# Attention into two MoE layers on one core: the inverse row sums reach the transposed layout as columns written by GpSimd and whole transpositions, in place of broadcast products

## The chip, the cores and the metric

The kernel runs on one core of one Trainium2 chip. The metric is the device time of one execution in microseconds (us), the median of several runs; lower is better. The names of the engines in the profile are PE (TensorE), DVE (VectorE), ACT (ScalarE), POOL (GpSimd) and SP (SyncE, which only issues transfers here).

## The reference

Three layers follow each other. A thresholded softmax attention over 4 batches, 8 heads, 576 positions and 64 channels feeds a mixture of experts (top 2 of 8), and that feeds a second one (top 1 of 8, with a skip). Only the attention is touched:

```
scores = scale * np.matmul(q, k.transpose(0, 1, 3, 2))
thresh = np.max(scores, axis=-1, keepdims=True) - tau
scores = np.where(scores >= thresh, scores, -1000000000.0)
scores = scores - np.max(scores, axis=-1, keepdims=True)
attn = np.exp(scores)
attn = attn / (np.sum(attn, axis=-1, keepdims=True) + 1e-09)
return np.matmul(attn, v).astype(np.float32)
```

## The kernel before

**Tiling of the attention.** Two heads form a pair, 16 pairs g in all, each with queries in tiles of 128 rows. A unit is one tile of one head, the fifth and last unit-tile holds the last 64 queries of both heads ("mixed"). Chunk c = 0 of a pair has four units, chunk c = 1 has five: nine units a pair, 144 in all. The loop over units is written by hand, as a software pipeline, and every engine executes what it is given in that order.

**One unit.** PE multiplies queries and keys into the score tile `s` (L290, issued two units ahead; three such tiles exist). DVE takes the negated maximum (L298), ACT the exponential (L300), DVE thresholds and sums (L329, tile `P`, or `Pm` for the mixed unit, with the sums at the side). PE transposes the 512 first keys of `P` in four pieces into the one PSUM tile `tp` (L339), which ACT copies to `pt` (L341, for the mixed unit L343). As there is one `tp` tile, the next transpositions wait until that copy is done.

**The end of a chunk.** A chunk of two tiles and two heads has four sums a row, five with the mixed unit. DVE reduces them (L348, `sums1`) and inverts them one unit later (L352, `sums2`). Two units after the chunk's last one, PE does `extra` (L357 to L365): the last 64 keys of both heads stand side by side in columns 512 to 640 of `P`, and are transposed together (L362); the inverse sums have to stand along the columns, so PE multiplies a broadcast inverse sum with the identity (L364, two halves of 64 output rows for each tile). ACT copies both into `rr` (L365). For c = 1 `extra_mixed` (L367 to L375) does the same for the mixed unit, in the `tp` tile, with four products of 64 columns and one ACT copy (L375). Then the products with the values (L386, `av` for four pieces of keys, L389 for the last keys) sum into the PSUM tile `x`, and DVE multiplies by the inverse sums (L396, `norm`).

**What sets the order.** The tables `AV` and `NORM` (L731 to L733) give, for each chunk, the unit and the phase ("mid", "pe", "end") in which the parts of `av` and `norm` are issued. Beside the units, generators are advanced one step at a time: `prep` (POOL multiplies the keys of a later pair by the scale, L273, when their transfer has landed), the router of the first MoE layer (`gate1`), whose results POOL scatters row by row to DRAM (L169, each after a small memset L168), and gathers for the first experts (L177). There are three bursts of such scatters inside the attention: 8, 10 and 8 of them. After the attention come the expert layers (L607, L847), where POOL takes part of the weight splits and the scatters of the output.

Of the kernel before, what the change touches and what calls it, by code (L numbers as in the profile page):

```python
# [8 lines left out]
F32 = mybir.dt.float32  # L9
F32R = mybir.dt.float32r  # L10
I32 = mybir.dt.int32
AF = mybir.ActivationFunctionType
# [5 lines left out]
B, H, S, D = 4, 8, 576, 64  # L18
# [21 lines left out]
def attention_moe_moe(ctx, tc, qT, kT, vm, vr, tau, wgn, noise, w1a, w2a, wsg, w1b, w2b, out):  # L40
    nc = tc.nc
# [11 lines left out]
    ident = const.tile([128, 128], F32, name="ident")  # L53
# [148 lines left out]
    def pool(stack, name, bufs, side="left", **kw):  # L202
        return stack.enter_context(tc.tile_pool(name=name, bufs=bufs, side=side, reuse_waits="tile", **kw))
# [13 lines left out]
    e_p = pool(actx, "e", 3, "right")  # L217
    pt_p = pool(actx, "pt", 2, "right")
    sm_p = pool(actx, "sm", 4, "right")
# [5 lines left out]
    def bank(nm):  # L225
        return banks[0](nm)
# [53 lines left out]
    chunk = {}  # L280
# [31 lines left out]
    def emit_stt(u):  # L312
        g, c, t, hh = UNITS[u]
        s, nm, e, th = st.pop(u)
        if (g, c) not in chunk:
            ch = chunk[g, c] = {}
            ch["pt"] = pt_p.tile([128, 4, 2, 320], F32, name="pt")
            ch["rr"] = pt_p.tile([128, 2, 320], F32, name="rr")
            ch["sums"] = smz[(2 * g + c) % 3]
            ch["P"] = {}  # L320
        ch = chunk[g, c]
        if t < 4:
            if hh == 0:
                ch["P"][t] = e_p.tile([128, 2 * S], F32, name="P", bufs=4)
            o, a = ch["P"][t][:, hh * S:(hh + 1) * S], ch["sums"][:, (t % 2) * 2 + hh, 0:1]
        else:
            ch["P"][t] = e_p.tile([128, S], F32, name="Pm", bufs=1)
            o, a = ch["P"][t], ch["sums"][:, 4, 0:1]
        nc.vector.scalar_tensor_tensor(o.rearrange("p (a b) -> p a b", a=2), s, th, e, op0=OP.is_ge, op1=OP.mult,  # L329
                                       accum_out=a)  # L330

# [16 lines left out]
        nc.vector.tensor_reduce(ch["sm"][:, :4 + c], ch["sums"][:, :4 + c], axis=AX.X, op=OP.add)  # L348

    def sums2(g, c):  # L350
        sm = chunk[g, c]["sm"][:, :4 + c]
        nc.vector.reciprocal(sm, sm)  # L352

    def wide(g, c, k):
        return chunk[g, c]["sm"][:, k:k + 1].to_broadcast([128, 64])

    def extra(g, c):  # L357
        ch = chunk[g, c]
        ps = ps_x.tile([128, 2, 256], F32, name="ex", tag="x")
        for i in range(2):  # L360
            cols = slice(i * 128, (i + 1) * 128)
            nc.tensor.transpose(ps[:, 0, cols], ch["P"][2 * c + i][:, 512:640], ident)  # L362
            for hh in range(2):
                nc.tensor.matmul(ps[hh * 64:(hh + 1) * 64, 1, cols], wide(g, c, 2 * i + hh), ident, start=True, stop=True)  # L364
        nc.scalar.activation(ch["rr"][:, :, 0:256], ps, AF.Copy)  # L365

    def extra_mixed(g):  # L367
        ch = chunk[g, 1]
        rr = ch["rr"]
        ps = bank("em").rearrange("p (k c) -> p k c", k=4)  # L370
        for i, l in enumerate((ch["P"][4][:, 512:S], wide(g, 1, 4))):
            for hh in range(2):
                h = slice(hh * 64, (hh + 1) * 64)
                nc.tensor.matmul(ps[h, i, 0:64], l, ident[:, h], start=True, stop=True)
        nc.scalar.activation(rr[:, :, 256:320], ps[:, 0:2, 0:64], AF.Copy)  # L375

    def av(g, c, kt):
        b, p = PAIRS[g]
# [345 lines left out]
    def early_mm1(k):  # L724
        if k < AHEAD:
            drain(products(e0a, k, ps_s.tile([128, 2, 512], F32, name="s")))
        if 0 < k <= AHEAD:
# [1 line left out]


    AV = (((3, "pe"), (3, "pe"), (4, "pe"), (4, "end"), (5, "pe")),  # L731
          ((3, "pe"), (3, "pe"), (4, "mid"), (4, "pe"), (5, "pe")))
    NORM = ((7, "mid"), (6, "pe"))  # L733
    pq.append(prep(1))
    for u in range(NU):
        g, c, t, hh = UNITS[u]
# [27 lines left out]
        run(u, "pe")  # L764
        run(u, "end")
        emit_stt(u)
        step(pq)
        step(bg)
        if u % 4 == 3:
            step(fq)  # L770
        if (t, hh) == ((1, 1) if c == 0 else (4, 0)):
            k = (g, c)
            sums1(*k)
            at(u + 1, "mid", sums2, *k)
            at(u + 2, "pe", extra, *k)
            if c:
                at(u + 2, "pe", extra_mixed, g)
            for kt, (d, ph) in enumerate(AV[c]):
                at(u + d, ph, av, *k, kt)
            at(u + NORM[c][0], NORM[c][1], norm, *k)  # L780
            if k in GATES:
                at(u + 7, "end", bg.append, gate_and_rows(*GATES[k]))
                if k[0] == 11:
                    at(u + 7, "end", bg.append, early_rows(e1a, 1))
# [711 lines left out]
```

## Time and profile before

| | |
|---|---|
| runs, median (lowest to highest) | 1089.65 us (1088.76 to 1092.91) |
| profiled execution, its own time | 1089.27 us |
| its span in the trace | 1087.5 us |
| PE busy in the span | 1015.5 us (93%) |
| DVE, ACT, POOL busy | 583.0 us, 490.4 us, 288.0 us |

Busy time counts an instruction from its start to its modelled end; TensorE's instructions overlap, so a busy PE has no room that this number shows. Where the text gives what a group of PE instructions costs, it goes by starts: from the first start of the group to the first start of what follows. A plain fp32 product shows as two records, a transposition as one. In the timeline a row merges instructions of one kind that follow each other.

### The profile page before, as it was taken

The page shows a single profiled execution, that of the slowest core. Times are in us where ns is not written, and L with a number is a line of the kernel's source. Part 1 is how long each engine was busy: PE and PEld are TensorE (multiplying, and loading weights), DVE is VectorE, ACT ScalarE, POOL GpSimd, SP SyncE. Part 2 cuts the span into 40 slices and gives each one's busy share as a digit, 9 for nine tenths or more (in the row PEclk, how much of TensorE's full clock was granted, in tenths as well). Part 3 has the DMA queues.
Part 4 walks back from the last instruction along what each step waited for, and adds up shares of the span by engine and source line. Part 5 has one row for each costly group of instructions (what it writes and reads, how often), then busy time and mean ns, then how long its engine had stood idle before and what let it go on. Part 6 is the DMA issues. An engine that isn't in the chain of part 4 may idle for free. (4 is left out here: it accounts for less than half of the span.)

```text
span 1087.5 us, 17417 instructions
## 1 busy us (share of the span) xinstructions
PE 1015.5 (93%) x6550; PEld 788.6 (73%) x6550; DVE 583.0 (54%) x1480; ACT 490.4 (45%) x925; POOL 288.0 (26%) x353
## 2 busy tenths in 40 slices
PE   6999999999998898999999999999998967899995
PEld 3555554555554786898989898989887747798894
DVE  6877787687776572453324242423324325666453
ACT  4666655565665452343333333333333213555352
POOL 3212033115204434231212212221222456223110
PEclk9999999999999998999999999999999978999998
DMA  6334262244420373544544445252454432566550
GB/s 147 101 86 118 96 169 58 58 130 88 155 79 1 126 208 103 136 132 104 142 107 130 113 113 133 74 161 70 101 180 168 163 104 71 199 214 205 173 227 15
DMA packets 54857, 134.78 MB, mean 124 GB/s; under 512 B 20043, under 2 KB 26475, under 8 KB 46064
## 3 DMA queue, kind: packets, MB, share of 16 engines
q1 hardware_dynamic: 41344, 107.17, 31.5%
q0 software_dynamic: 13424, 26.45, 11.2%
q8 instruction: 53, 0.87, 0.4%
q14 instruction: 36, 0.29, 0.1%
HBM read 112.64 MB, written 23.69 MB: 125 GB/s over the span
## 5 line engine op out<-in xcount | busy, mean ns | idle before, releaser
L621 DVE SCALAR_TENSOR_TENSOR hl<-h,hh 128x128 fp32r<-128x128 f32 (+3 forms) x157 | 80.2, 511 | 177.2 <-ACT hh L620 158.7
L847 PE MATMUL y<-w2h,hh 128*128 128x512 f32 x418 | 171.3, 410 | 0.0
L847 PE MATMUL y<-w2l,hh 128*128 128x512 f32 x418 | 164.7, 394 | 4.0 <-DVE w2l L816 4.0
L847 PE MATMUL y<-w2h,hl 128*128 128x512 f32 x418 | 165.3, 395 | 0.0
L620 ACT ACTIVATE hh<-h 128x128 fp32r<-128x128 f32 (+3 forms) x157 | 71.4, 455 | 198.3 <-PE h L607 146.2
L607 PE MATMUL h<-xh,w1h 128*128 128x320 f32 (+2 forms) x596 | 154.0, 311 | 3.7 <-ACTq L976 1.5
L607 PE MATMUL h<-xl,w1h 128*128 128x320 f32 (+2 forms) x596 | 152.4, 308 | 1.3 <-DVE xl L590 1.3
L607 PE MATMUL h<-xh,w1l 128*128 128x320 f32 (+2 forms) x596 | 151.8, 307 | 0.0
L298 DVE TENSOR_REDUCE nm<-s 128x1 f32<-128x576 f32 x144 | 108.8, 756 | 61.5 <-PE s L290 54.3
L290 PE MATMUL s<-kr,qr 64*128 64x288 f32 (+1 forms) x640 | 112.6, 462 | 8.4 <-DVE kr L273 5.3
L300 ACT ACTIVATE e<-s,nm 128x576 f32<-128x576 f32 x144 | 106.1, 737 | 15.2 <-DVE nm L298 11.8
L341 ACT ACTIVATE pt<-tp 128x512 f32<-128x512 f32 x128 | 76.5, 597 | 80.8 <-PE tp L339 70.1
L607 PEld LDWEIGHTS h<-xh,w1h 128*128 128x128 f32 x596 | 105.0, 190 | 6.1 <-ACTq L976 1.9
L607 PEld LDWEIGHTS h<-xl,w1h 128*128 128x128 f32 x596 | 105.3, 190 | 2.5 <-DVE xl L590 2.4
L329 DVE SCALAR_TENSOR_TENSOR P<-s,th,e 128x576 f32<-128x576 f32 x128 | 103.5, 809 | 3.9
L607 PEld LDWEIGHTS h<-xh,w1l 128*128 128x128 f32 x596 | 105.6, 191 | 0.0
L856 POOL DMA_INDIRECT out_dram<-yo,tid x35 | 55.4, 1583 | 173.6 <-ACT yo L855 93.0
L339 PEld LDWEIGHTS tp<-ident,P 128*128 128x128 f32 x512 | 54.8, 142 | 59.3 <-issue 18.1
L847 PEld LDWEIGHTS y<-w2l,hh 128*128 128x128 f32 x418 | 79.7, 191 | 19.3 <-DVE w2l L816 5.2
L847 PEld LDWEIGHTS y<-w2h,hl 128*128 128x128 f32 x418 | 79.3, 190 | 17.7
L273 POOL TENSOR_SCALAR kr<-kr,qsc 128x288 f32<-128x288 f32 x45 | 44.9, 1006 | 174.7 <-DMA kr<-in_kT_dram 174.3
L339 PE MATMUL tp<-ident,P 128*128 128x128 f32 x512 | 85.3, 290 | 5.8 <-DVE xl L590 2.8
(267 smaller groups left out, 1490.9 us busy)
## 6 DMA issues: line engine op xcount, KB each, us to landing
rw<-in_w1a_dram SPq DMA_DIRECT2D x18, 1024.0 KB
rw<-in_w2a_dram SPq DMA_DIRECT2D x18, 1024.0 KB
qr<-in_qT_dram SPq DMA_DIRECT2D x30, 288.0 KB
rw<-in_w1b_dram SPq DMA_DIRECT2D x8, 1024.0 KB
rw<-in_w2b_dram SPq DMA_DIRECT2D x8, 1024.0 KB
kr<-in_kT_dram SPq DMA_DIRECT2D x96, 72.0 KB
out_dram<-zx SPq DMA_DIRECT2D x9, 512.0 KB
x<-xr SPq DMA_DIRECT2D x18, 256.0 KB
```

Of the source, the lines that this page charges most:

```text
L273: eng.tensor_scalar(kr[:, j], kr[:, j], qsc, None, op0=OP.mult)
L290: nc.tensor.matmul(s[o, i, 0:SH], qr[r, h, t * 128:min((t + 1) * 128, S)], kr[r, h if t < 4 else 2 * h], start=True, stop=True)
L298: nc.vector.tensor_reduce(nm, s, axis=AX.XY, op=OP.max, negate=True)
L300: nc.scalar.activation(e, s, AF.Exp, bias=nm)
L329: nc.vector.scalar_tensor_tensor(o.rearrange("p (a b) -> p a b", a=2), s, th, e, op0=OP.is_ge, op1=OP.mult, accum_out=a)
L339: nc.tensor.transpose(ps[:, kt], P[:, c0 + kt * 128:c0 + (kt + 1) * 128], ident)
L341: nc.scalar.activation(ch["pt"][:, :, hh, (t % 2) * 128:(t % 2 + 1) * 128], ps, AF.Copy)
L607: nc.tensor.matmul(ps[:, c, 0:m], w[:, kd, :], v[:, kd, a:a + m], start=(kd == 0 and j == 0), stop=(kd == KD - 1 and j == 2))
L620: nc.scalar.activation(dh, src, AF.Relu)
L621: nc.vector.scalar_tensor_tensor(dl, src, 0.0, dh.bitcast(F32), op0=OP.max, op1=OP.subtract)
L847: nc.tensor.matmul(y, h[:, i * 128:(i + 1) * 128], w, start=(f == 0 and j == 0), stop=(f == KF - 1 and j == 2))
L856: nc.gpsimd.indirect_dma_start(out=x2[:, :], out_offset=bass.IndirectOffsetOnAxis(ap=tid, axis=0), in_=yo, in_offset=None, compute_op=OP.a ...
```

## The change

`sums2`, which inverted the sums, now also lets POOL write them out: a new tile `rb` of 128 rows and 6 by 64 columns, in which each inverse sum fills 64 columns (one copy of 256 columns for the four sums of a chunk; for c = 1 another of 128 columns for the mixed unit). For c = 1 POOL also copies the last 64 columns of `Pm` to 64 new columns behind it, so that these keys stand there twice. In `extra` each pair of broadcast products gives way to one transposition of 128 columns of `rb`; in `extra_mixed` four products of 64 columns give way to two transpositions of 128 columns, and as their result stands at different columns for the two heads, one ACT copy becomes two, of 64 rows each. In the table `AV`, the third part of `av` for c = 1 moves from the phase "mid" to the phase "pe" of the same unit.

```diff
         else:
-            ch["P"][t] = e_p.tile([128, S], F32, name="Pm", bufs=1)
-            o, a = ch["P"][t], ch["sums"][:, 4, 0:1]
+            ch["P"][t] = e_p.tile([128, S + 64], F32, name="Pm", bufs=1)
+            o, a = ch["P"][t][:, 0:S], ch["sums"][:, 4, 0:1]
...
     def sums2(g, c):
-        sm = chunk[g, c]["sm"][:, :4 + c]
+
+        ch = chunk[g, c]
+        sm = ch["sm"][:, :4 + c]
         nc.vector.reciprocal(sm, sm)
-
-    def wide(g, c, k):
-        return chunk[g, c]["sm"][:, k:k + 1].to_broadcast([128, 64])
+        ch["rb"] = sm_p.tile([128, 6, 64], F32, name="rb", bufs=2)
+        nc.gpsimd.tensor_copy(ch["rb"][:, 0:4], ch["sm"][:, 0:4, None].to_broadcast([128, 4, 64]))
+        if c:
+            nc.gpsimd.tensor_copy(ch["rb"][:, 4:6], ch["sm"][:, 4:5, None].to_broadcast([128, 2, 64]))
+            nc.gpsimd.tensor_copy(ch["P"][4][:, S:S + 64], ch["P"][4][:, S - 64:S])
...
             nc.tensor.transpose(ps[:, 0, cols], ch["P"][2 * c + i][:, 512:640], ident)
-            for hh in range(2):
-                nc.tensor.matmul(ps[hh * 64:(hh + 1) * 64, 1, cols], wide(g, c, 2 * i + hh), ident, start=True, stop=True)
+            nc.tensor.transpose(ps[:, 1, cols], ch["rb"][:, 2 * i:2 * i + 2].rearrange("p a b -> p (a b)"), ident)
...
-        for i, l in enumerate((ch["P"][4][:, 512:S], wide(g, 1, 4))):
-            for hh in range(2):
-                h = slice(hh * 64, (hh + 1) * 64)
-                nc.tensor.matmul(ps[h, i, 0:64], l, ident[:, h], start=True, stop=True)
-        nc.scalar.activation(rr[:, :, 256:320], ps[:, 0:2, 0:64], AF.Copy)
+        nc.tensor.transpose(ps[:, 0], ch["P"][4][:, S - 64:S + 64], ident)
+        nc.tensor.transpose(ps[:, 1], ch["rb"][:, 4:6].rearrange("p a b -> p (a b)"), ident)
+        for hh in range(2):
+            h = slice(hh * 64, (hh + 1) * 64)
+            nc.scalar.activation(ch["rr"][h, :, 256:320], ps[h, 0:2, h], AF.Copy)
...
-          ((3, "pe"), (3, "pe"), (4, "mid"), (4, "pe"), (5, "pe")))
+          ((3, "pe"), (3, "pe"), (4, "pe"), (4, "pe"), (5, "pe")))
```

On PE the program stands as follows around the end of the second chunk of pair 0: `ex` and `em` are the PSUM tiles of `extra` and `extra_mixed`, `sm` the inverse sums, `x4` the number of instructions of the program. Before:

```order
L362 MATMUL ex<-ident,P 128x128
L364 MATMUL ex<-ident,sm 64x128 x2
L374 MATMUL em<-ident,Pm 64x64 x2
L374 MATMUL em<-ident,sm 64x64 x2
L290 MATMUL s<-kr,qr 128x288 x2
L339 MATMUL tp<-ident,P 128x128 x4
L386 MATMUL x<-pt,v 64x320 x4
L290 MATMUL s<-kr,qr 128x288 x2
L386 MATMUL x<-pt,v 64x320 x2
L339 MATMUL tp<-ident,P 128x128 x4
L386 MATMUL x<-pt,v 64x320 x2
```

On PE at the same place in the changed kernel, where the lines after the new ones are three higher:

```order
L367 MATMUL ex<-ident,P 128x128
L368 MATMUL ex<-ident,rb 128x128
L374 MATMUL em<-ident,Pm 128x128
L375 MATMUL em<-ident,rb 128x128
L290 MATMUL s<-kr,qr 128x288 x2
L339 MATMUL tp<-ident,P 128x128 x4
L389 MATMUL x<-pt,v 64x320 x4
L290 MATMUL s<-kr,qr 128x288 x2
L339 MATMUL tp<-ident,P 128x128 x4
L389 MATMUL x<-pt,v 64x320 x4
```

Products became transpositions one for two, and the value products of the next unit but one now all stand behind the transpositions of their unit.

On POOL the end of the second burst of scatters, in pair 11, stands as follows before (`slots` is the table in DRAM, `kr` the keys of a later pair):

```order
L168 MEMSET spacer 1x1
L169 DMA slots_60<-mt_2851,ii_2874 18432x2
L168 MEMSET spacer 1x1
L169 DMA slots_60<-mt_2865,ii_2906 18432x2
L273 TENSOR_SCALAR kr<-kr,qsc 128x288 x3
L177 DMA xs<-x_62,gid 128x512 x2
```

And on POOL at the same place in the changed kernel, where the first three copies are those of chunk (11, 1) and the fourth that of chunk (12, 0):

```order
L168 MEMSET spacer 1x1
L169 DMA slots_60<-mt_2864,ii_2887 18432x2
L168 MEMSET spacer 1x1
L169 DMA slots_60<-mt_2878,ii_2917 18432x2
L356 COPY rb<-sm 128x256
L358 COPY rb<-sm 128x128
L359 COPY Pm<-Pm 128x64
L356 COPY rb<-sm 128x256
L273 TENSOR_SCALAR kr<-kr,qsc 128x288 x3
```

The copies of chunk (11, 1) stand behind all ten scatters of this burst. In the first and in the third burst one copy, that of chunk (7, 0) and of chunk (15, 0), stands behind four of the eight.

## Rows read from the trace of the kernel before

**Rows 1.** Page: busy time, share of the span and instructions of PE
```profile
PE 1015.5 (93%) x6550; PEld 788.6 (73%) x6550; DVE 583.0 (54%) x1480; ACT 490.4 (45%) x925; POOL 288.0 (26%) x353
```

**Rows 2.** Windows: stretch, its length, busy time by engine, granted clock, DMA
```profile
20.00:320.00 300.00, 293.07 (x2142) 157.73 (x2141) 231.16 (x658) 186.94 (x326) 63.08 (x80) 0.99 0.39 107
...
349.60:355.50 5.90, 5.88 (x26) 4.57 (x26) 2.02 (x8) 1.82 (x3) 0.00 (x0) 0.51 0.04 1
```

**Rows 3.** Timeline, PE, end of a first chunk: start, length, operation [idle before]
```profile
60.35 0.66 PE L339 MATMUL tp<-ident,P 128*128 128x128 f32 x4
60.84 0.27 PE L362 MATMUL ex<-ident,P 128*128 128x128 f32 x1
...
62.04 0.71 PE L290 MATMUL s<-kr,qr 64*64 64x288 f32 x8
```

**Rows 4.** Timeline, PE, end of the next second chunk
```profile
70.81 0.27 PE L362 MATMUL ex<-ident,P 128*128 128x128 f32 x1
...
72.23 0.76 PE L290 MATMUL s<-kr,qr 64*128 64x288 f32 x4
72.94 0.66 PE L339 MATMUL tp<-ident,P 128*128 128x128 f32 x4
73.53 1.30 PE L386 MATMUL x<-pt,v 128*64 128x320 f32 x8
74.75 0.76 PE L290 MATMUL s<-kr,qr 64*128 64x288 f32 x4
75.44 0.76 PE L386 MATMUL x<-pt,v 128*64 128x320 f32 x4
...
77.41 0.76 PE L290 MATMUL s<-kr,qr 64*128 64x288 f32 x4
```

**Rows 5.** Timeline, ACT, the same place
```profile
71.01 0.60 ACT L341 ACTIVATE pt<-tp 128x512 f32<-128x512 f32 x1
72.12 0.60 ACT L365 ACTIVATE rr<-ex 128x512 f32<-128x512 f32 x1 [0.52 <-PE ex L364]
72.62 0.27 ACT L375 ACTIVATE rr<-em 128x128 f32<-128x128 f32 x1
72.77 0.74 ACT L300 ACTIVATE e<-s,nm 128x576 f32<-128x576 f32 x1
```

**Rows 6.** Timeline, DVE, the same place
```profile
68.08 0.18 DVE L352 RECIPROCAL sm<-sm 128x5 f32<-128x5 f32 x1
```

**Rows 7.** Groups on POOL: line engine op xcount | busy, mean ns | idle before
```profile
L273 POOL TENSOR_SCALAR kr<-kr,qsc 128x288 f32<-128x288 f32 x45 | 44.9, 1006 | 174.7 <-DMA kr<-in_kT_dram 174.3
```

**Rows 8.** Timeline, POOL, start of the program
```profile
2.75 0.52 POOL L513 MEMSET zx<- 128x512 f32 x1
```

**Rows 9.** Timeline, all engines, the second burst of scatters
```profile
254.91 1.02 POOL L169 DMA_INDIRECT slots<-mt,ii  x1 [13.50 <-DVE ii L477]
...
261.93 0.18 DVE L352 RECIPROCAL sm<-sm 128x5 f32<-128x5 f32 x1
...
265.38 0.27 PE L362 MATMUL ex<-ident,P 128*128 128x128 f32 x1
...
268.49 0.66 PE L339 MATMUL tp<-ident,P 128*128 128x128 f32 x4 [0.93 <-issue]
268.93 0.97 POOL L169 DMA_INDIRECT slots<-mt,ii  x1 [0.21 <-issue]
```

**Rows 10.** Timeline, PE, end of the attention
```profile
349.62 1.97 PE L386 MATMUL x<-pt,v 128*64 128x256 f32 x8 [3.00 <-ACT rr L365]
```

**Rows 11.** Timeline, POOL and PE, fourth scatter of the first burst, and what follows
```profile
159.82 0.97 POOL L169 DMA_INDIRECT slots<-mt,ii  x1 [0.22 <-issue]
...
166.43 0.33 PE L362 MATMUL ex<-ident,P 128*128 128x128 f32 x1 [0.68 <-issue]
```

**Rows 12.** Timeline, POOL, fourth scatter of the third burst
```profile
341.65 0.97 POOL L169 DMA_INDIRECT slots<-mt,ii  x1 [0.21 <-issue]
```

**Rows 13.** Timeline, PE, shortly behind it
```profile
344.11 0.27 PE L362 MATMUL ex<-ident,P 128*128 128x128 f32 x1
```

More of the change, by code (lines that the diff above doesn't have):

```diff
@@ L368, in extra_mixed @@
         ch = chunk[g, 1]
-        rr = ch["rr"]
         ps = bank("em").rearrange("p (k c) -> p k c", k=4)
-        for i, l in enumerate((ch["P"][4][:, 512:S], wide(g, 1, 4))):
-            for hh in range(2):
-                h = slice(hh * 64, (hh + 1) * 64)
-                nc.tensor.matmul(ps[h, i, 0:64], l, ident[:, h], start=True, stop=True)
-        nc.scalar.activation(rr[:, :, 256:320], ps[:, 0:2, 0:64], AF.Copy)
+        nc.tensor.transpose(ps[:, 0], ch["P"][4][:, S - 64:S + 64], ident)
[3 more added lines that the diff above has]
+            nc.scalar.activation(ch["rr"][h, :, 256:320], ps[h, 0:2, h], AF.Copy)
     def av(g, c, kt):
```

## The prediction

> **What bounds the kernel now.** I read the page first: PE is busy for 93% of the span, DVE for 54%, ACT for 45%, POOL for 26% [rows 1]. The change lies in the attention, so that stretch counts, and there the windows say the same more sharply: from 20 to 320 us PE is busy for 293.1 of 300 us at a granted clock of 0.99, DVE for 231.2, ACT for 186.9, POOL for 63.1 [rows 2]. A time saved on PE's queue is therefore a time gained, until another engine's chain is late. What PE pays for a group I take from the timeline by starts, since the lengths of its records overlap. Four transpositions (L339) start at 60.35 and the next group at 60.84: 0.49 us, so 0.12 each; followed by products of another shape four take 0.59 (72.94 to 73.53), so the turn costs 0.10 [rows 3, 4].
>
> **Extra, first chunk.** From 60.84 to 62.04, 1.20 us, PE does two transpositions and four products of 64 output rows [rows 3]. Afterwards it is four transpositions, 0.59. Gain 0.61 a chunk, 16 chunks.
>
> The Trainium skill (TensorE: Matmul & The Clock Gate, section Part 4: PE-mode transpose) gives about 275 ns for a 128 by 128 transposition inside a kernel. The trace agrees as far as the record goes, 0.27 us for one of L362 [rows 3], and disagrees as to what the queue pays, 0.12. By the page's figure as an estimate four would cost 1.10 and nearly nothing would be gained; the measurement decides here, and what remains is a rival below.
>
> **Extra, second chunk.** From 70.81 to 72.23 stand the same group and the mixed unit's four small products, 1.42 us [rows 4]. Afterwards six transpositions: 6 x 0.12 + 0.10 = 0.83. By PE alone the gain would be 0.59. But the mixed result lies in the one `tp` tile, and the next transpositions (L339 at 72.94) wait until ACT has emptied it: L375 ends at 72.89 [rows 5]. I lay this chain out from the start of `extra`. A copy starts 0.20 after PE leaves its group (L341 at 71.01, PE at 70.81), and a copy of 0.60 holds ACT for 0.50 (L365 to L375). So L365 starts at 0.70 (PE would allow 0.69, ACT comes from L341 at 0.70), the first small copy at 1.20, the second, new one 0.15 later (the step from L375 to L300) and ends at 1.62; PE goes on at 1.67. Before it was 72.94 - 70.81 = 2.13. Gain 0.46 a chunk: the second ACT copy and the copy L365 ahead of it take the rest.
>
> **The moved value products.** In the third unit of that chunk PE does four records of `av`, four transpositions, four records of `av` from 75.44 to 77.41: 1.97 us. Its neighbour, with the transpositions first and eight records in one run, takes 0.59 (72.94 to 73.53) + 1.22 (73.53 to 74.75) = 1.81 [rows 4]. Gain 0.16. What the transpositions need, the tile `P` of the unit before, is two units old by DVE's order, so nothing becomes late by it.
>
> **POOL's copies, where POOL is free.** A copy from a broadcast column does not occur before. The nearest rows bound its rate: multiplying 288 columns takes 1.006 us, 3.5 ns a column [rows 7], setting 512 columns takes 0.52 us, 1.0 ns a column [rows 8]. The 256 columns then take 0.26 to 0.89 us; I take 0.6, nearer to L273, which reads SBUF as the copy does. All three copies of a second chunk, 448 columns, take 0.46 to 1.56. They start when the inversion ends, 68.26 [rows 6], so the first is done by 69.2 and the last by 69.8. PE wants the first at its second transposition, 70.81 + 0.12, and the last at 70.81 + 0.49 = 71.30. Margin 1.5 us at least, cost nothing. If this cover went, each us would be a us of PE. The key scaling L273 that now stands between copies waits only for transfers that landed long before: POOL sits idle 174.3 us for them, ahead of need [rows 7].
>
> **POOL's copies behind scatters.** POOL is in order, and a scatter takes some 1.3 us from start to start. In the second burst all ten stand ahead of the copies of chunk (11, 1). The first starts at 254.91, when its indices are ready; the last starts at 268.93 and ends at 269.90 [rows 9]. With 0.6 for the copy, `rb` is there at 270.5 (270.2 to 270.8). PE's second transposition of that chunk stood at 265.38 + 0.12, and comes 0.61 earlier by the gain of chunk (11, 0) at the start of the burst: 264.9. The inversion itself was done at 262.11, so POOL's queue is what PE waits for: 5.6 us. PE stood idle for 0.93 us at 268.49 before [rows 9], and I let that wait fall into the new one: 4.7 us. Then comes the clock. After PE waited 3.00 us at 349.62 [rows 10], its granted clock was 0.51 for 5.90 us, which is the lower level, 1.2 GHz [rows 2]; at 2.4 GHz this work takes 3.0, so the fall cost 2.9. For the new, longer wait I take 2.5 (0 if the clock holds, 2.9 as there). Together 7.2 us, between 4.4 and 7.9.
>
> In the first burst the copy of chunk (7, 0) stands behind four scatters, the fourth of which ends at 160.79, and PE wants it after 166.43 [rows 11]; even 1.2 us earlier by the gains there are over 3 us left. In the third, the fourth scatter ends at 342.62 [rows 12], the copy by 342.9 to 343.5, and PE wants it at 344.11 + 0.12 [rows 13], less 0.46 + 0.16 gained since the burst's start: 343.6. That is tight; I count nothing, and half a us at most. What is queued behind a waiting copy, scatters and key scaling, is late by the wait, and nobody needs it within pairs. DVE's instructions are the same; ACT has 16 small copies more, hidden except where they are counted above.
>
> **The sum.** 16 x (0.61 + 0.46 + 0.16) = 19.7 us gained, 7.2 lost in one place: 12.5 us. From the profiled execution's 1089.27 us this leaves 1076.8, and as that execution lies 0.4 below the median, I say 1077 for the time to compare with 1089.65. The expert layers follow when the attention ends; their first weights are loaded in a stretch in which DMA is hardly used (0.04 of its time from 349.6 to 355.5, rows 2), so I expect them to move up with it.
>
> **Rivals.**
> First, the burst does not hold PE: the scatters come early enough or the copy gets past. Against it stands the order, in which POOL cannot pass them. Time 1089.3 - 19.7 = 1069.6. Chance 0.13.
>
> Second, PE's room is not filled: DVE, busy for 77% of the stretch [rows 2], and the single `tp` tile become the bound in the units around `extra`, and half of the gain is given back: 1089.3 - 9.9 + 7.2 = 1086.6. For it: DVE's share would rise to about 82%, with short units in which PE has less to do than DVE. Against it: three score tiles let PE and DVE drift by two units. Chance 0.20.
>
> Third, the burst's wait comes twice more, in the first and the third, as the margin of the third is small: 1076.8 + 2 x 7.2 = 1091.2. Chance 0.05.
>
> Fourth, on the other side: POOL's copies from broadcast columns are slow everywhere. In a second chunk they have 3.0 us, from 68.26 to 71.30. From 3.8 us, 8.5 ns a column, 16 waits of 0.8 eat the whole 12.5; at three times the rate of L273, 4.7 us, 16 x 1.7 = 27 us are lost, 1104. Against it: nothing on POOL in these rows is that slow. Chance 0.04.
>
> Fifth, each transposition holds PE for its record of 0.27: a first chunk gains 1.20 - 1.08 = 0.12, a second loses 0.20 and gains 0.16, 1.3 us in all, and the burst costs 7.2: 1095. It is the page's figure turned into a mechanism; the groups of four in 0.49 [rows 3] speak against it. Chance 0.03.
>
> **How the numbers follow.** The forecast, 1077, has 0.55. Its own range is 1073 to 1082, by the burst's bounds and two or three us of small waits. For 8 in 10 I reach down to the first rival and up to the second: 1068 to 1088. A measurement of this kernel tells about 0.5%, 5.4 us, from no change. Faster by more than that: the forecast, the first rival and a part (0.07) of the second, 0.75. Within it: the rest of the second and the third, 0.18. Slower: the fourth and the fifth, 0.07.
>
> **What would show it.** In the trace after: `extra` of a first chunk takes 0.6 us from start to start, that of a second 1.67 until the transpositions of the next unit, with two ACT copies ahead of them; the unit with the moved products takes 1.8; a copy of 256 columns on POOL takes 0.26 to 0.89; and near 255 to 270 us less the gain so far PE waits some 5 us for POOL, with a clock near 0.5 behind it. I am wrong if that wait is missing or comes in other places too, if transpositions of `rb` cost more than 0.12 each, or if PE shows new idle time behind DVE in the units around `extra`.

## The result, and the profile after

The changed kernel takes 1074.73 us (median of 4 runs, 1071.83 to 1077.79), the kernel before beside it on the same chip 1090.71 us (1088.76 to 1092.91). The ratio is 0.985, with a 95% interval of 0.982 to 0.989: some 16 us less, between 12 and 20. Forecast were 1077 and a range of 1068 to 1088. The profiled execution is the slowest of the four, 1077.79 us with a span of 1076.0, which is 11.5 less than the span before. Of the four, the two slower ones (1077.79 and 1076.12) have a mean granted clock of 0.976, the two faster ones (1071.83 and 1073.34) 0.978 and 0.979. Both traces have the same length behind the attention, from the first product into the tile `h` of the first expert layer on: 716.22 us (1087.5 - 371.28) before and 716.31 us (1076.0 - 359.69) after. So the whole difference between these two traces, 11.5 us, lies in the attention; the rest of the 16 us lies between executions and is not explained by them.

First the page after, the line that answers to [rows 1]:

```profile
PE 993.1 (92%) x6262; PEld 780.3 (73%) x6262; DVE 581.4 (54%) x1480; ACT 494.6 (46%) x941; POOL 306.7 (29%) x417
```

PE has 288 instructions and 22.4 us less, POOL 64 (32 copies of 256 columns, 16 of 128 and 16 of 64) and 18.7 us more. The windows after, with the same columns as [rows 2]; the second and third stretch are the place in the second burst of scatters:

```profile
20.00:320.00 300.00, 280.04 (x1932) 154.73 (x1932) 236.48 (x678) 194.44 (x348) 79.52 (x136) 0.99 0.40 107
259.00:262.00 3.00, 2.90 (x11) 1.82 (x12) 0.27 (x1) 1.77 (x4) 0.45 (x3) 0.50 0.01 0
262.00:266.00 4.00, 4.00 (x28) 2.02 (x26) 2.83 (x10) 2.00 (x4) 0.38 (x1) 0.94 0.71 216
```

In the same 300 us PE is busy for 280 instead of 293, and DVE for 236 instead of 231: PE now has idle time, though no other engine is near full. Where that idle time lies is the subject of the rest.

**End of a first chunk, and of a second.** PE's timeline after, answering to [rows 3] and, from 68.09 on, to [rows 4]; columns are start, length, operation, and in brackets the idle time before and what ended it:

```profile
58.80 0.27 PE L367 MATMUL ex<-ident,P 128*128 128x128 f32 x1
58.91 0.27 PE L368 MATMUL ex<-ident,rb 128*128 128x128 f32 x1
...
59.33 0.71 PE L290 MATMUL s<-kr,qr 64*64 64x288 f32 x8
...
68.09 0.27 PE L367 MATMUL ex<-ident,P 128*128 128x128 f32 x1
...
68.42 0.27 PE L368 MATMUL ex<-ident,rb 128*128 128x128 f32 x1
69.03 0.30 PE L374 MATMUL em<-ident,Pm 128*128 128x128 f32 x1 [0.34 <-ACT pt L341]
69.17 0.27 PE L375 MATMUL em<-ident,rb 128*128 128x128 f32 x1
69.37 0.76 PE L290 MATMUL s<-kr,qr 64*128 64x288 f32 x4
70.09 0.66 PE L339 MATMUL tp<-ident,P 128*128 128x128 f32 x4
...
72.59 0.66 PE L339 MATMUL tp<-ident,P 128*128 128x128 f32 x4
73.17 1.30 PE L389 MATMUL x<-pt,v 128*64 128x320 f32 x8
74.40 0.76 PE L290 MATMUL s<-kr,qr 64*128 64x288 f32 x4
```

`extra` of the first chunk is 0.53 from start to start (58.80 to 59.33) where it was 1.20. The unit with the moved value products is 1.81 (72.59 to 74.40) where it was 1.97. At the second chunk's end, from the start of `extra` to the next transpositions it is 2.00 (68.09 to 70.09) where it was 2.13, and in it stands a wait of 0.34 that was not there before: L374 writes into the `tp` tile and waits for the copy of the transpositions that went before it. This wait of 0.34 stands in 13 of the 16 pairs, not in pairs 10, 11 and 15. ACT at that place, answering to [rows 5]:

```profile
68.29 0.60 ACT L341 ACTIVATE pt<-tp 128x512 f32<-128x512 f32 x1
68.79 0.59 ACT L369 ACTIVATE rr<-ex 128x512 f32<-128x512 f32 x1
69.48 0.56 ACT L378 ACTIVATE rr<-em 64x128 f32<-64x128 f32 x2
```

**POOL's copies.** The view by source for L356, the copy of 256 columns, with its durations and who waited for it in the whole program:

```profile
L356 POOL COPY rb<-sm x32: 397/401/416, 19.4 to 350.7; 128x256 f32<-128x256 f32 x32
...
  PE ex L368: 4.8, 1
```

401 ns for 256 columns, and PE waits for it once in 32 times. That once is the second burst, PE first and POOL in a fence of its own:

```profile
254.04 0.27 PE L367 MATMUL ex<-ident,P 128*128 128x128 f32 x1
259.10 0.47 PE L368 MATMUL ex<-ident,rb 128*128 128x128 f32 x1 [4.78 <-POOL rb L356]
...
260.35 1.33 PE L290 MATMUL s<-kr,qr 64*128 64x288 f32 x4
...
266.35 0.76 PE L290 MATMUL s<-kr,qr 64*128 64x288 f32 x4
```

```profile
257.66 0.97 POOL L169 DMA_INDIRECT slots<-mt,ii  x1 [0.21 <-issue]
258.63 0.41 POOL L356 COPY rb<-sm 128x256 f32<-128x256 f32 x1
258.98 0.30 POOL L358 COPY rb<-sm 128x128 f32<-128x128 f32 x1
259.21 0.24 POOL L359 COPY Pm<-Pm 128x64 f32<-128x64 f32 x1
```

The copy starts when the tenth scatter ends, and PE 0.06 after the copy. Behind the wait the granted clock is 0.50, the 1.2 GHz level (second line of the windows): a score unit takes 1.33 at 260.35 where it takes 0.76 at 266.35.

**By stretch.** Adding up from one start of `extra` to another, in the traces of before and after. PE's timeline before, and then after; the starts at 265.38 and 344.11 (before) and at 254.04 (after) stand above:

```profile
21.74 0.27 PE L362 MATMUL ex<-ident,P 128*128 128x128 f32 x1
...
275.99 0.27 PE L362 MATMUL ex<-ident,P 128*128 128x128 f32 x1
...
362.74 0.33 PE L362 MATMUL ex<-ident,P 128*128 128x128 f32 x1 [1.26 <-DVE xT L396]
...
371.28 0.39 PE L607 MATMUL h<-xh,w1h 128*128 128x256 f32 x1
```

```profile
21.60 0.27 PE L367 MATMUL ex<-ident,P 128*128 128x128 f32 x1
...
269.34 0.27 PE L367 MATMUL ex<-ident,P 128*128 128x128 f32 x1
...
335.12 0.27 PE L367 MATMUL ex<-ident,P 128*128 128x128 f32 x1
...
351.83 0.33 PE L367 MATMUL ex<-ident,P 128*128 128x128 f32 x1 [1.26 <-DVE xT L399]
...
359.69 0.38 PE L610 MATMUL h<-xh,w1h 128*128 128x256 f32 x1
```

| stretch | before | after | gained | forecast |
|---|---|---|---|---|
| up to `extra` of chunk (0,0) | 21.74 | 21.60 | 0.14 | 0 |
| to `extra` of (11,1), 23 chunks | 243.64 | 232.44 | 11.20 | 14.14 |
| to (12,0), the second burst | 10.61 | 15.30 | -4.69 | -6.58 |
| to (15,0), 6 chunks | 68.12 | 65.78 | 2.34 | 3.69 |
| to (15,1), the third burst | 18.63 | 16.71 | 1.92 | 0.61 |
| to the first product into `h` | 8.54 | 7.86 | 0.68 | 0.62 |
| sum | 371.28 | 359.69 | 11.59 | 12.48 |

### The profile page after: what moved, and what is told of

Read it like the earlier page. It is cut to its first block, busy times and chain, and to the rows that moved or that the text cites. A ratio compares the mean times of both kernels' runs of the same rounds, so it can differ in the third digit from the quotient of the medians.

```text
span 1076.0 us, 16952 instructions
## 1 busy us (share of the span) xinstructions
PE 993.1 (92%) x6262; PEld 780.3 (73%) x6262; DVE 581.4 (54%) x1480; ACT 494.6 (46%) x941; POOL 306.7 (29%) x417
## 5 line engine op out<-in xcount | busy, mean ns | idle before, releaser
L341 ACT ACTIVATE pt<-tp 128x512 f32<-128x512 f32 x128 | 76.5, 598 | 76.1 <-PE tp L339 65.5
L339 PEld LDWEIGHTS tp<-ident,P 128*128 128x128 f32 x512 | 54.6, 142 | 58.6 <-issue 15.4
L850 PEld LDWEIGHTS y<-w2h,hh 128*128 128x128 f32 x418 | 79.6, 190 | 16.2 <-ACT w2h L818 1.6
```

The source lines that it names most:

```text
L339: nc.tensor.transpose(ps[:, kt], P[:, c0 + kt * 128:c0 + (kt + 1) * 128], ident)
L341: nc.scalar.activation(ch["pt"][:, :, hh, (t % 2) * 128:(t % 2 + 1) * 128], ps, AF.Copy)
L850: nc.tensor.matmul(y, h[:, i * 128:(i + 1) * 128], w, start=(f == 0 and j == 0), stop=(f == KF - 1 and j == 2))
```

## Experiments

The theory after the result: (a) in nearly every pair PE is now held by ACT's copy of the `tp` tile (0.34 us), so that the second chunk gains little; (b) one wait for POOL, in the second burst, takes back about 6 us; (c) POOL's copies are hidden everywhere else. The rivals: that the copies cost more than shown, on whatever engine; that the second small ACT copy, not the tile, holds PE; that a wait taken away comes back elsewhere. Each ratio is to the kernel before, run beside it on the same chip. Since the expert layers, which no variant touches, took from 706.5 to 716.4 us in these traces, I take sizes below some 5 us from the stretches of a trace, not from totals. "The attention" of a trace is the stretch from its first steady score product, near 13 us, to the first product into `h`.

**1. The copies of one chunk on DVE.**

```diff
-        nc.gpsimd.tensor_copy(ch["rb"][:, 0:4], ch["sm"][:, 0:4, None].to_broadcast([128, 4, 64]))
+        eng = nc.vector if (g, c) == (11, 1) else nc.gpsimd
+        eng.tensor_copy(ch["rb"][:, 0:4], ch["sm"][:, 0:4, None].to_broadcast([128, 4, 64]))
...
```

The two other copies are changed likewise.

> The changed kernel, with the three copies of chunk (11, 1) alone done by DVE instead of POOL, so that they don't stand behind the ten scatters. Theory (PE is the bound and POOL's queue holds it in one place): the wait of 4.78 us at L368 goes, the clock does not fall behind it, and the first expert product, at 359.7 us in the changed kernel's trace, comes 4 to 6 us earlier. Rival (the wait only covers another one, since DVE stood still for 3.65 us at that place before the change): a wait of 3 us or more appears on DVE or PE right behind, and at most 1 to 2 us are gained.

Measured: 1066.49 us (1061.90 to 1069.79), ratio 0.984 (0.981 to 0.987). PE's timeline at the burst:

```profile
256.07 0.27 PE L368 MATMUL ex<-ident,P 128*128 128x128 f32 x1
256.18 0.27 PE L369 MATMUL ex<-ident,rb 128*128 128x128 f32 x1
...
262.32 0.76 PE L290 MATMUL s<-kr,qr 64*128 64x288 f32 x4
```

From `extra` to the third score unit behind it are 6.25 us where the changed kernel needs 12.31 (254.04 to 266.35): the wait and the slow stretch behind it cost 6.06, and nothing stands in their place there. So the order on POOL is the cause of that wait, not the copy. The first product into `h` comes 7.1 earlier than in the changed kernel (352.59 against 359.69), more than the 4 to 6 expected: the third burst, which this edit does not touch, is 3.05 shorter in this trace (13.66 against 16.71 from (15,0) to (15,1)). A second run of the same kernel:

> The changed kernel with the copies of chunk (11, 1) on DVE, once more, beside the two others. Theory: the attention as in its first trace, 338.9 us, within 1.5; ratio to the kernel before 0.980 to 0.984.

1067.20 us (1065.39 to 1070.56), ratio 0.984 (0.982 to 0.987); the stretch from (11,1) to (12,0) is 9.24 both times, against 15.30. The attention missed what was expected, 336.62 in place of 338.9 within 1.5, as the first burst took 1.63 less (11.86 against 13.49 from (7,0) to (7,1)). The totals fall by less than those 6 us against the changed kernel (0.9839 and 0.9843 against 0.9853 and, below, 0.9867, which is 1 to 3 us), but their intervals are 5 to 8 us wide, and cannot tell the two apart. Experiment 4, on the chip of the first run, keeps the burst's wait (15.91 in that stretch) and has the same total, 1067.08; its expert layers are 5.9 shorter in the trace (706.49 against 712.41). So the 6 us are shown in the attention; that the whole program is shorter by as much is not shown.

**2. The mixed transpositions one unit later, at its end.**

```diff
-                at(u + 2, "pe", extra_mixed, g)
+                at(u + 3, "end", extra_mixed, g)
```

> The changed kernel, with the mixed unit's two transpositions one unit later, behind the value products of the next unit. Theory (they wait 0.34 us for ACT to empty the tp tile in all 16 pairs, because extra became so short that it no longer covers this copy): the wait at L374 goes, from the start of extra to the next transpositions it takes 1.3 us instead of 2.0, the two transpositions cost 0.25 to 0.35 at their new place, 0.35 to 0.45 a pair are gained, 6 to 7 us in all. Rival (the two ACT copies hold the next transpositions wherever they stand): the wait turns up at the transpositions of the unit behind, 0.3 us or more each, and nothing is gained.

Measured: 1070.44 us (1065.87 to 1073.95), ratio 0.988 (0.984 to 0.991). PE's timeline at the former place, and in a unit in which the router works:

```profile
68.06 0.76 PE L290 MATMUL s<-kr,qr 64*128 64x288 f32 x4
68.75 0.66 PE L339 MATMUL tp<-ident,P 128*128 128x128 f32 x4
...
109.67 0.66 PE L408 MATMUL tr<-ident,xT 128*128 128x128 f32 x4 [0.65 <-ACT rr L378]
```

The 0.34 is gone in all pairs, and the second chunk, from the score unit behind the mixed transpositions to that behind its last value products, takes 8.99 (66.28 to 75.27) instead of 9.38 (66.84 to 76.22 in the changed kernel): the wait was what (a) says. But the router's instructions at the end of a unit now wait 0.65 for the small copies in five places (109.67, 194.43, 217.18, 237.46 and 284.95; one such wait, at 191.87, stands in the changed kernel). The attention as a whole is 2 us shorter than in the changed kernel (344.46 against 346.48), not the 6 of 16 x 0.39, and these 2 lie in the third burst (14.12 against 16.71). From `extra` of (0,0) to that of (15,0) it takes 313.57 against 313.52: there all is given back, 2.6 us of it in four more of the router's waits; where the rest goes is not shown.

**3. The moved value products alone, on the kernel before.**

```diff
-          ((3, "pe"), (3, "pe"), (4, "mid"), (4, "pe"), (5, "pe")))
+          ((3, "pe"), (3, "pe"), (4, "pe"), (4, "pe"), (5, "pe")))
```

> The kernel before, with only the table of the value products changed (the third part of c = 1 in phase pe). Theory: the unit takes 1.81 instead of 1.97 us, 16 x 0.16 = 2.6 us faster than before. Rival: the transpositions, now 0.69 us earlier, wait for P or for the tp tile, and nothing is gained (0 to 0.5 us).

Measured: 1081.78 us (1079.50 to 1085.47), ratio 0.998 (0.996 to 1.000). PE's timeline:

```profile
76.12 0.66 PE L339 MATMUL tp<-ident,P 128*128 128x128 f32 x4
77.93 0.76 PE L290 MATMUL s<-kr,qr 64*128 64x288 f32 x4
```

1.81 from 76.12 to 77.93, as forecast; the pair is 0.14 shorter, the attention 3.0 us (354.93 against 357.94). This part is worth 2 to 3 of the 16 us by the trace; the ratio alone does not tell it from nothing.

**4. The mixed unit by products, as before, the rest as changed.** The two small copies on POOL go, the four products and the single ACT copy come back.

```diff
-        nc.tensor.transpose(ps[:, 0], ch["P"][4][:, S - 64:S + 64], ident)
-        nc.tensor.transpose(ps[:, 1], ch["rb"][:, 4:6].rearrange("p a b -> p (a b)"), ident)
...
+                nc.tensor.matmul(ps[h, i, 0:64], l, ident[:, h], start=True, stop=True)
+        nc.scalar.activation(rr[:, :, 256:320], ps[:, 0:2, 0:64], AF.Copy)
```

> The changed kernel, with the mixed unit done as before (four small products, one ACT copy, two POOL copies less); extra keeps its transpositions. Theory (the mixed unit waits for the tp tile whatever its instructions are): the wait of 0.34 us stays, and the time is that of the changed kernel within 2 us. Rival (the prediction's chain: the second ACT copy sets when PE goes on): 0.15 us a pair earlier, 2.4 us faster than the changed kernel, and the first expert product 2.4 us earlier.

Measured: 1067.08 us (1066.21 to 1068.19), ratio 0.985 (0.981 to 0.989), that of the changed kernel. PE's timeline:

```profile
69.31 0.34 PE L375 MATMUL em<-ident,Pm 128*64 128x64 f32 x4 [0.25 <-ACT pt L341]
...
69.69 0.76 PE L290 MATMUL s<-kr,qr 64*128 64x288 f32 x4
70.38 0.66 PE L339 MATMUL tp<-ident,P 128*128 128x128 f32 x4
```

The products wait for the same copy. With one ACT copy instead of two the second chunk, measured as in 2, is 0.09 shorter (9.29). Between the score unit behind the mixed unit and the next transpositions, where the second copy could hold PE, are 0.69 (69.69 to 70.38) in place of 0.72 (69.37 to 70.09): 0.03 of the 0.09. So the rival, 0.15 by the second copy, falls, and the mixed unit's part of the change gains nothing.

**5. The changed kernel again, on the chip of the next three.**

> The changed kernel once more, in one call with its variants. Theory: the same stages as in the trace shown (18.60 us a pair in the steady stretch, a wait of about 4.8 us for POOL in the second burst), and a ratio to the kernel before of 0.985, within the interval measured, 0.982 to 0.989.

Measured: 1075.31 us (1072.54 to 1077.60), ratio 0.987 (0.983 to 0.990). The trace is the same: 0.34 before L374, 4.81 before L368 in the second burst, an attention of 346.21.

**6. All copies on DVE.** As in 1, with `eng = nc.vector` for every chunk.

> The changed kernel, with all copies done by DVE instead of POOL. Theory (PE is the bound, DVE has some 20% of room): DVE's extra 0.8 us or so a pair is hidden, the pair stays at 18.6 us, and the one wait for POOL goes: 5 to 7 us faster than the changed kernel. Rival (DVE is all but the bound in the units around extra, so that only POOL makes the change worthwhile): 0.3 us or more a pair are lost there, 5 us in all, and the gain is used up.

Measured: 1071.91 us (1070.46 to 1072.84), ratio 0.984 (0.981 to 0.987). PE's timeline in the unit before `extra`:

```profile
66.65 0.66 PE L339 MATMUL tp<-ident,Pm 128*128 128x128 f32 x4
67.52 0.76 PE L290 MATMUL s<-kr,qr 64*128 64x288 f32 x4 [0.21 <-DVE P L329]
```

The burst's wait is gone, and a new one of 0.2 to 0.4 comes behind DVE in nine places. DVE's busy time from 20 to 320 us is 249.7 (236.5 in the changed kernel). A steady pair with this wait is 0.15 to 0.18 longer than in the changed kernel (18.75 to 18.78 against 18.60), the one without it 0.07 shorter (18.53). One cancels part of the other: between the medians of 5 and of this run, on one chip, are 3.4 us, not the 5 to 7 expected. GpSimd isn't needed for the gain; what it takes off DVE is worth 1 to 2 us (9 x 0.15), and its queue loses 6 in one place.

**7. Every copy on POOL three times.**

```diff
+        for _ in range(3):
+            nc.gpsimd.tensor_copy(ch["rb"][:, 0:4], ch["sm"][:, 0:4, None].to_broadcast([128, 4, 64]))
...
```

> The changed kernel, with each set of POOL's copies done three times, 0.7 to 2.5 us more on POOL a chunk. Theory (the copies are hidden, with a margin of over 1.5 us): no wait of PE for POOL over 0.1 us in the steady stretch, 18.6 us a pair, and the wait of the second burst longer by 0.7 us at its first copy. Rival (the copies are on the path already): 0.7 us or more a pair longer.

One run: 1074.89 us. The second chunk's length is unchanged (66.76 to 76.14, 9.38), so with 2.3 us of copies instead of 0.8 in a second chunk PE still doesn't wait there: (c) holds with room. PE waits for POOL in two places only:

```profile
261.11 0.48 PE L369 MATMUL ex<-ident,rb 128*128 128x128 f32 x1 [6.26 <-POOL rb L357]
...
352.25 0.33 PE L369 MATMUL ex<-ident,rb 128*128 128x128 f32 x1 [0.55 <-POOL rb L357]
```

The wait in the burst is 1.5 longer, twice the 0.7 expected: the third copy of 256 columns starts 1.51 after the first (260.67 and 259.16), since the small ones stand between them. What is queued ahead on POOL counts there, one for one.

**8. The mixed result in the `x` tile.** To take the mixed unit out of `tp`, its products go into free columns of the tile `x` that `av` fills later, one unit later and ahead of `av`; so POOL's two small copies go, and the copy of (11,1) is on DVE as in 1.

```diff
-        ps = bank("em").rearrange("p (k c) -> p k c", k=4)
+        ch["x"] = ps_x.tile([128, 512], F32, name="x")
+        ps = ch["x"][:, 320:448].rearrange("p (k c) -> p k c", k=2)
...
-                at(u + 2, "pe", extra_mixed, g)
+                at(u + 3, "pe", extra_mixed, g)
```

> The changed kernel, with the mixed unit's four small products put into the free columns of the tile x, one unit later ahead of the value products, where no tp tile is needed, and the copy of chunk (11, 1) on DVE. Theory: neither the wait for the tp tile nor ACT's copies hold PE: 0.35 us a pair less than the changed kernel (18.25 us), 5.6 us in all, and 6 us from the burst: 11 to 12 us faster than the changed kernel, ratio to before 0.974 to 0.977. Rival (DVE or the exponentials become the bound when PE is this short): the pair stays above 18.45 us.

Measured: 1075.47 us (1072.88 to 1079.69), ratio 0.987 (0.984 to 0.991), no faster than the changed kernel in 5. PE's timeline:

```profile
70.94 0.29 PE L376 MATMUL x<-ident,sm 128*64 128x64 f32 x4
71.70 1.30 PE L388 MATMUL x<-pt,v 128*64 128x320 f32 x8 [0.47 <-ACT rr L377]
```

In 15 of the 16 pairs `av` waits for ACT to have read the other columns of the same tile, 0.47 in most of them, 0.38 to 0.94 in all. The wait ends on ACT, not on DVE, which was the rival. The wait for a copy was carried from one tile to another.

**9. The same, with the products before the transpositions of the unit** ("mid" in place of "pe" in the last line of 8), so that these transpositions lie between the products and `av`.

> As the variant with the mixed unit's products in the free columns of x and the copy of chunk (11, 1) on DVE, but with these products ahead of the transpositions of that unit, so that ACT's copy of them runs beside the transpositions and not ahead of the value products. Theory: the wait of 0.47 us at the value products goes, what is left is 0.1 us for ACT's copy of extra; 18.3 us a pair against 18.60 of the changed kernel; the attention 9 to 11 us shorter than in the changed kernel (335 to 338 us from the first steady product to the first expert product, where that one has 346.3). Rival (the tile x, like tp, makes PE wait for ACT wherever the products stand): a wait of 0.3 us or more appears at the products or behind them, and the pair stays at 18.6.

Measured: 1061.88 us (1060.45 to 1064.26), ratio 0.979 (0.9765 to 0.9815), the best of all, with an interval that ends just below that of the changed kernel (0.9817 to 0.9890). PE's timeline:

```profile
68.07 0.76 PE L290 MATMUL s<-kr,qr 64*128 64x288 f32 x4
68.88 0.34 PE L376 MATMUL x<-ident,Pm 128*64 128x64 f32 x4
69.05 0.29 PE L376 MATMUL x<-ident,sm 128*64 128x64 f32 x4
69.26 0.66 PE L339 MATMUL tp<-ident,P 128*128 128x128 f32 x4
```

Between the scores and the products about 0.1 is lost, and nothing behind them: the second chunk takes 9.10 (66.29 to 75.39) in place of 9.38. That makes 4.5 us over 16 pairs, and its median lies 5.3 below that of its neighbour in 1, taken again on the same chip. In the one trace, though, the attention is no shorter than there (340.09 against 336.62, where 335 to 338 were expected): the stretches from `extra` of (7,0) to (7,1) and of (15,0) to (15,1), both in bursts of scatters, take 14.03 and 16.47 where the neighbour takes 11.86 and 13.70, and behind its waits of 2.96 and 2.58 the granted clock shows 0.64 and 0.57 over 4 us, 1.00 in the neighbour. The gain a pair is shown; why the totals show it whole is not, as the expert layers in that trace are 6.3 us shorter (708.29 against 714.54). Their granted clock was at the lower level for 34 us there and for 44 in the neighbour; the instructions in them are the same, and whether the change has a part in that clock was not tested.

**10. Experiments 1 and 2 together.**

> The changed kernel, with the mixed unit's transpositions one unit later and the copies of chunk (11, 1) on DVE, both together. Theory (the two gains add, less the waits of 0.65 us in units with router work that the late transpositions bring): the attention 8 to 9 us shorter than in the changed kernel, 337 to 339 us. Rival (one hides the other): 340 us or more.

Measured: 1066.52 us (1064.15 to 1069.36), ratio 0.984 (0.981 to 0.986), that of 1 alone. The attention takes 339.54, between the theory and the rival; 1 alone took 338.90 and 336.62. As in 2, what the late transpositions gain a pair is given back.

## Why the prediction was right, and by which steps it was not

**In the traces the gain came out 0.9 us below the forecast, 11.59 against 12.48, by errors that offset each other**: the gain a pair was put 0.27 too high, 4.3 us in all; the loss in the burst about 2 too high; and the third burst gave 1.3 more than was counted. That they nearly cancel is luck. The median lies 2 us on the other side of the forecast, and the profiled execution 3 us above the median, so this pair of traces doesn't explain those 2.

- *Extra, first chunk*: 0.61 forecast, 0.67 measured. The two kinds of transposition follow each other at 0.11. The Trainium skill's 275 ns (TensorE: Matmul & The Clock Gate, Part 4: PE-mode transpose), given there beside a bf16 figure, fits the record of these fp32 transpositions, 0.27, here as before; for what the queue pays the trace stays with less than half of it, and the fifth rival is out.
- *Extra, second chunk*: 0.46 forecast, 0.13 measured. This is the step that failed. I laid ACT's chain out with the one `tp` tile as a limit on what comes after the mixed unit, and missed that it limits the mixed unit's own entry as well: "six transpositions" cannot follow each other, as the last two write the tile that L341 is still reading. Before, the transpositions and products of `extra` held PE for 1.10 from 70.81 on, and the copy was over by 71.61 [rows 4, 5]; it was the work that the change removes which hid it. Up to L369 the chain runs as laid out (0.20 and 0.70 behind `extra`); the small copy then starts at 1.39 and not at 1.20, and PE goes on at 2.00 and not 1.67. Experiments 2 and 4 show the tile as the cause, and leave the new second copy at most 0.09, of which 0.03 stand where it could hold PE.
- *The moved value products*: 0.16 forecast, 0.16 measured; alone 0.14 (experiment 3).
- *A pair*: 1.23 forecast, 0.96 measured (19.56 to 18.60); over 16 pairs 15.4 in place of 19.7.
- *POOL's copies where POOL is free*: right. 401 ns lie in the bounds of 0.26 to 0.89, below the 0.6 taken; three times the copies still cost nothing in a steady pair (experiment 7).
- *POOL's copies behind scatters*: the place, the mechanism and the level of the clock were right. The wait was 4.78 in place of 5.6: the copy took 0.41 and not 0.60, and PE did not arrive earlier against the scatters, since from `extra` of (11,0) to that of (11,1) PE takes 10.92 after and 10.99 before. The term mis-sized most was the clock's, 2.5: with 4.78 of wait and 6.06 for both, it cost 1.3. It was sized after the fall at the end of the attention, where PE worked 5.74 us at the lower level (to 355.36); here it worked 3.4, from 259.10 to 262.5. The fall itself was as long both times, 6.8 us, but here half of it lay in the wait, where PE had no work to slow down.
- *The first and third burst*: no wait, as forecast. The copy of (7,0) ends at 154.71 and PE wants it at 157.22; that of (15,0) ends at 334.11 for 335.23. The margin in the third, 1.1, is wider than the 0.1 to 0.7 that I read: the copy is short, and `extra` comes no earlier against the fourth scatter, 1.43 behind its end (1.49 before, [rows 12, 13]). The 1.3 us more than forecast in that stretch stand beside the clock behind the wait there: 0.51 over 5.90 us before [rows 2], 0.57 from 341 to 345 after; that the clock is their cause is not shown, as the variants differ by more there (last section).
- *The rivals*: of the second, that PE's room is not filled, a part came true, with ACT's tile and not DVE as the holder. The first is what experiment 1 makes of the kernel; in the attention it is worth 6 and not 7.2. The third did not come, as PE waits for POOL in one place only, nor the fourth, with 401 ns for 256 columns (1.6 ns a column).

## What to carry to other kernels

When work on the bound engine is shortened, look at what it covered at both ends: a single buffer that was free in time, because the removed work lay between its two users, becomes the wait. Small helper work on an idle engine is only free where that engine's queue is free; list what stands ahead of it at each place in the program, and give the one bad place to another engine. Moving a result to another tile helps only if PE has other work there between writing the result and its next write into that tile, long enough for the copy to be read out.

## What the runs showed that I had not expected

- At the ends of the scatter bursts ACT and DVE stand still for 2 to 4 us, before and after the change, and PE behind them. In the changed kernel ACT's timeline shows in the first burst:

```profile
160.92 0.60 ACT L341 ACTIVATE pt<-tp 128x512 f32<-128x512 f32 x1 [3.86 <-remote]
```

  The rows name no instruction as the releaser, the length differs between traces of one kernel (the same stretch took 11.86 and 13.49 in the two traces of experiment 1), and the cause stays open; nothing was tried on it. In the third burst, the stretch from (15,0) to (15,1) took 13.42 to 14.12 in six of the thirteen traces and 16.10 to 18.63 in the seven others, before and after among them; a kernel that only does POOL's copies three times (experiment 7) has 13.42. So what that stretch gained in the table isn't shown to be the change's.
- A GpSimd copy takes 401 and 296 ns for 256 and 128 columns from a broadcast column (L356, L358) and 238 ns for 64 plain columns (L359): about 0.18 us and 0.9 ns a column, a quarter of the 3.5 ns a column that L273 shows [rows 7].
- A longer wait of PE was not followed by a longer time at the lower clock: 3.4 us behind 4.78, 5.74 behind 3.00 [rows 10], and none behind the 3.21 of the first burst after (granted 1.00 from 161.5 to 169.5), though the clock fell behind 2.58 in experiment 9. In the first two the granted clock was 0.50 for the same 6.8 us (255.69 to 262.51 after, 348.54 to 355.36 before), and what differs is how much of that lay in the wait: 3.4 and 1.1.
- The expert layers, the same in every variant, took 706.5 to 716.4 us, and a part of that goes with the clock: behind the first product into `h` it was at the lower level for 32 to 34 us in the traces with 706.49, 708.29 and 711.31, and for 42 to 44 in those with 714.54 to 716.44. Ten us at half the clock account for 5 us at most, so it is not the whole. This compares traces; no run tests it.
